# An attention and MLP kernel on one core: the first batch's attention in another order, the second batch's memory keys transposed early, one weight load cut in two

## The chip, the cores and the metric

The kernel runs on one core of a Trainium2 chip. The metric is device time in microseconds (us). Five engines work side by side, each through its own list of instructions in order, and they meet at semaphores only: TensorE (PE, with its weight loads shown as PEld), VectorE (DVE), ScalarE (ACT), GpSimd (POOL) and SyncE (SP). ACT, POOL and SP also issue DMAs, each on a queue of its own.

## The reference

Attention over chunks of 32 queries, each with 16 positions of left context, 8 of right context and 8 memory rows, for 4 batches, 8 heads, 768 positions, 64 values a head; then an MLP of 512 to 2048 to 512 with a "snake" function on the 3072 rows.

```python
for c in range(nc):                       # chunks of 32
    k_full = np.concatenate([mem_k, k_ctx], axis=2)
    v_full = np.concatenate([mem_v, v_ctx], axis=2)
    a = softmax(scale * q_c @ k_full.T)   # scale = 1/8
    out[:, :, c_start:c_end] = a @ v_full
x = out.transpose(0, 2, 1, 3).reshape(B * S, H * D)
h = x @ w_in
s = np.sin(alpha * h)
return (h + s * s / (alpha + 1e-09)) @ w_out
```

## The kernel before

All work is written out by hand in the tuple WORDS: five strings, one for the front and one for each of the four batches. A word is a letter and a number; method `do_<letter>` of the class Stage emits the instructions, and the order of the words is the order of the instructions on every engine. String 0 is the front: batch 0's attention alone. String i (from 1) is the MLP of batch i-1 with the attention of batch i woven in.

Words of the front that matter here, by head pair 0 to 3:

- `a` casts an f32 piece of q or k to bf16. Numbers 0 to 3 are k, 4 to 7 are q; the last letter is the engine, A for ACT (L700) and V for DVE (a tensor_tensor that takes the maximum of the piece with itself, L698). Pieces 0, 1, 2 of both come by ACT's and SP's queues (`load_f`, L762); piece 3 of both comes already cast by POOL's queue (`d`, L192).
- `l` and `k` transpose a q or k piece on PE into a bank of PSUM (12 instructions, L313); `L` and `K` copy it out on the named engine (L333, L324) and give the bank back.
- `s` is the scores of a head pair and half of the positions on PE (L351, L359), then their exponential on ACT (L366). `v` is the values (PE, L378), then the reciprocal of the sum and the product on DVE (L387, L388), which leave a tile x_blk.
- `T` and `t` transpose an x_blk on PE (L400) and copy it to xT, the MLP's input, on ACT (`T`) or DVE (`t`) (L403).
- `z` is one dummy matmul of 512 columns on PE (L733), `y` four of 128 columns (L739). `Ws` loads ACT's table for the sine (L752).
- `V`, `I`, `U`, `dq`, `dk`, `dm`, `dn` issue loads on POOL: values (L209, L216), w_in by tiles of 128 columns (L250), w_out (L256), the next batch's q and k (L192), memory values, and batch 1's memory keys (L713).
- `Ck` is const_k: 4 small PE transposes of the memory keys (L832), a copy to memkT (L836), and a copy into kT (L244). `n1` does the same for batch 1 later.

In the MLP strings `b` and `h` are the two halves of one of 16 tiles of the first layer (4 matmuls each, L462), `h` ends with the sine on ACT (L477), `q` squares it on the named engine (ACT L482, DVE and POOL L485), `g` finishes the tile on DVE (L489) and gives its two PSUM banks back, and `f` takes steps of the second layer (L500). `p0` and `P0` at the end of the front are the first three matmuls of the two halves of tile 0. PSUM has 8 banks of this kind, handed out in pairs or one by one by the class Banks as the words are run, so a PE instruction often waits for the engine that still reads its bank.

POOL's loads use eight semaphores in turn: each load waits until the one eight places ahead has landed.

Of the kernel before, what the change touches and what calls it, by code (L numbers as in the profile page):

```python
# [20 lines left out]

WORDS = (
    (
# [3 lines left out]
    ),  # L27
    (
# [93 lines left out]
def kernel(  # L122
# [12 lines left out]
    nc = tc.nc  # L135
# [5 lines left out]
    HP = H // 2  # L141
# [82 lines left out]
    def put_memv(b, eng=None):  # L224
        (eng or nc.vector.tensor_copy)(
            vws[b % 2][64:72, :, :, 0:D],
            memv_st[64:72, b, :, :].unsqueeze(2).to_broadcast([NM, H, NJ, D]),
        )
# [14 lines left out]
    def put_memk(b):  # L243
        nc.vector.tensor_copy(  # L244
            kTs[b % 2][:, :, 24:856].rearrange("p g (j c) -> p g j c", c=104)[:, :, :, 40:40 + NM],
            memkT[:, :, NM * b:NM * b + NM].unsqueeze(2).to_broadcast([P, HP, NJ, NM]),
        )
# [295 lines left out]
    class Stage:  # L543
# [137 lines left out]
        def do_m(self, a):  # L681
            put_memv(int(a))

        def do_n(self, a):
            const_k(int(a))

        def do_H(self, a):
            put_memv_heads(int(a))
# [67 lines left out]
    kq_f = [mlp.tile([P, 2, 6 * D], F32, name="kq_f", tag=t) for t in ("u", "s2") * 4]  # L756
# [4 lines left out]
    def load_f(ring, src, hp, t):  # L761
        ring.dma_start(  # L762
            t[:], src[0, 2 * hp:2 * hp + 2].rearrange("h (p r) d -> p h (r d)", p=P)
        )
# [3 lines left out]
    load_f(nc.sync, k, 0, kq_f[0])  # L768
    load_f(nc.scalar, q, 1, kq_f[HP + 1])
    nc.sync.dma_start(memk_f[0:NM], mem_k[0].rearrange("h n d -> n h d"))  # L770
    load_f(nc.scalar, q, 2, kq_f[HP + 2])
    load_f(nc.sync, k, 1, kq_f[1])
    load_f(nc.scalar, k, 2, kq_f[2])
    nc.sync.dma_start(alpha_rows[:], moe_alpha.rearrange("(ft p) -> ft p", p=P))
    nc.vector.memset(zeros[:], 0.0)
# [48 lines left out]
    def const_d():  # L824
        nc.vector.tensor_copy(memk_bf[0], memk_f[0:NM])

    def const_k(b=0):
        bank, bs = banks.single()
        a = memk_at[b]
        mt = bank[:, 0:2 * NM].bitcast(BF).rearrange("p (g c) -> p g c", g=HP)  # L830
        for g in range(HP):
            nc.tensor.transpose(  # L832
                mt[:, g, :], memk_bf[b][:, 2 * g:2 * g + 2, :].rearrange("p e d -> p (e d)"),
                ident[a:a + NM, a:a + NM]
            )
        nc.vector.tensor_copy(memkT[:, :, NM * b:NM * b + NM], mt)  # L836
        put_memk(b)
        banks.give(bs)

    def const_g():  # L840
        nc.vector.tensor_copy(memv_st[64:72, 0], memv_f[64:72])
# [22 lines left out]
    def const_s():  # L864
        nc.gpsimd.memset(kst[0:32, 0, :], 0.0)
        nc.gpsimd.memset(kst[96:128, NJ - 1, :], 0.0)

    consts_of = dict(b=const_b, d=const_d, g=const_g, c=const_c, m=const_m, i=const_i, k=const_k, l=const_l, p=const_p, v=const_v,
                     s=const_s, z=const_z)

# [36 lines left out]
```

## Time and profile before

| | |
|---|---|
| three runs | 213.85, 214.62, 214.97 us; median 214.62 |
| the profiled execution | 213.57 us, of which its span (first to last instruction) is 211.4 us |
| PE busy | 204.2 us (97%) |
| DVE, ACT, POOL busy | 139.6, 142.8, 100.7 us |
| POOL's queue of loads | 13.65 MB, 90.4% of the 16 DMA engines' time |
| first layer on PE (L462) | 512 matmuls, 326 ns each by the profile, one every 0.16 us |
| second layer on PE (L500) | 400 matmuls, 371 ns each by the profile |

A timeline row reads: start, length, engine, line, operation, output<-input, shapes, how many merged; in brackets the idle time of the engine ahead of it and what ended it. The times count from the span's start. A matmul's end is modelled: rows of matmuls overlap. In the rows of DMA issues the last number is the median time from issue to landing.

### The profile page before, as it was taken

Reading aid. Unit: us, or ns where it says so; the run is one execution under the profiler, and the core shown is the slowest. Engines: PE = TensorE matmul, PEld = TensorE weight load, DVE = VectorE, ACT = ScalarE, POOL = GpSimd, SP = SyncE. Lnnn points to the kernel's source line nnn. Section 1 sums busy time; section 2 is a strip of 40 time slices with the busy share of each in tenths; the row PEclk is TensorE's granted clock in tenths of the full one; section 3 lists DMA queues with packets and bytes.
Section 4 is the critical chain, followed back from the end, with each engine's and each line's share of the span. In section 5 each row is a group of like instructions: output and inputs, shape, how many; then the busy total and the mean of one; then the engine's idle time right before and its main releaser. Section 6 shows DMA issues by size and latency. Waiting matters only on the chain.

```text
span 211.4 us, 4539 instructions
## 1 busy us (share of the span) xinstructions
PE 204.2 (97%) x1754; PEld 116.8 (55%) x1754; DVE 139.6 (66%) x212; ACT 142.8 (68%) x228; POOL 100.7 (48%) x143
## 2 busy tenths in 40 slices
PE   7789999999999999999999999999999999999994
PEld 7467665656455555554456555554555555554443
DVE  7579698998363669957675569887347189964011
ACT  4499798959838579978827298968755198991110
POOL 8999518496696496029991058960000023300000
PEclk9999999999999999999999999999999999999999
DMA  6999999999999999999996569999246400000312
GB/s 212 308 138 137 211 207 203 205 163 178 167 162 131 165 142 150 99 142 157 159 201 120 82 175 133 131 137 88 102 105 109 136 0 0 5 0 0 149 53 99
DMA packets 95925, 27.81 MB, mean 132 GB/s; under 512 B 84880, under 2 KB 92448, under 8 KB 95904
## 3 DMA queue, kind: packets, MB, share of 16 engines
q0 software_dynamic: 69296, 13.65, 90.4%
q1 hardware_dynamic: 25520, 12.30, 29.7%
q10 hardware_dynamic: 1088, 1.57, 2.1%
q8 instruction: 14, 0.23, 0.5%
q14 instruction: 7, 0.06, 0.1%
HBM read 29.66 MB, written 6.29 MB: 170 GB/s over the span
## 4 chain that ended last, share of the span: by engine, by line
PE 83%; DVE 6%; ACT 4%; issue 2%; DMA 2%; POOL 1%; SPq 0%; DVEq 0%
PE ps L500 40%; PE ps L462 32%; PE ps L448 3%; PE ps L419 2%; PE ps L313 2%; DMA kq_f<-in_k_dram 2%; DVE gT L489 2%; DVE x_blk L388 2%; PE ps L400 1%; DVE s L485 1%; ACT u L477 1%; PE ps L733 1%; POOL s L485 1%; ACT s L482 1%; ACT pt L366 1%
## 5 line engine op out<-in xcount | busy, mean ns | idle before, releaser
L500 PE MATMUL ps<-w_out_sb,gT 128*128 128x512 bf16 (+2 forms) x400 | 89.0, 371 | 0.0
L462 PE MATMUL ps<-xT,w_in_sb 128*128 128x384 bf16 x512 | 86.4, 326 | 0.4 <-DVE gT L489 0.2
L489 DVE SCALAR_TENSOR_TENSOR gT<-s,inv_alpha,ps 128x768 bf16<-128x768 f32 x64 | 63.2, 1011 | 11.7 <-POOL s L485 5.3
L462 PEld LDWEIGHTS <-w_in_sb 128*128 128x128 bf16 x512 | 49.6, 98 | 35.4 <-issue 2.4
L477 ACT ACTIVATE u<-ps,alpha_sb 128x768 f32<-128x768 f32 x64 | 56.7, 896 | 18.1 <-PE ps L462 17.7
L500 PEld LDWEIGHTS <-gT 128*128 128x128 bf16 x400 | 36.6, 98 | 37.8 <-DVE gT L489 0.2
L485 POOL TENSOR_TENSOR s<-u 128x768 f32<-128x768 f32 x11 | 17.7, 1615 | 63.4 <-ACT u L477 50.8
L433 ACT ACTIVATE pt<-ps,biasm 128x256 bf16<-128x256 f32 x72 | 27.2, 490 | 10.5 <-PE ps L419 10.5
L507 DVE COPY o_sb<-ps 128x512 f32<-128x512 f32 (+1 forms) x15 | 10.1, 678 | 27.8 <-PE ps L500 25.9
L485 DVE TENSOR_TENSOR s<-u 128x768 f32<-128x768 f32 x24 | 22.8, 952 | 7.4 <-ACT u L477 7.4
L482 ACT ACTIVATE s<-u 128x768 f32<-128x768 f32 x29 | 24.2, 841 | 0.5
L388 DVE TENSOR_TENSOR x_blk<-ps,rinv 96x512 bf16<-96x512 f32 x32 | 22.0, 687 | 1.3 <-DVE rinv L387 0.2
L507 ACT COPY o_sb<-ps 128x512 f32<-128x512 f32 (+1 forms) x10 | 5.6, 562 | 22.2 <-PE ps L500 22.2
L387 DVE RECIPROCAL rinv<-ps 96x8 f32<-96x8 f32 x32 | 6.4, 199 | 13.3 <-PE ps L448 12.4
L209 POOL DMA_DIRECT2D vw<-in_v_dram x13 | 12.0, 923 | 5.1 <-PE ps L400 5.1
L216 POOL DMA_DIRECT2D vw<-in_v_dram x13 | 12.5, 958 | 1.1 <-issue 0.6
L275 POOL DMA_DIRECT2D kst<-in_k_dram x16 | 12.0, 748 | 1.6 <-DMA vw<-in_v_dram 0.7
L269 POOL DMA_DIRECT2D kst<-in_k_dram x16 | 11.1, 691 | 1.8 <-DMA vw<-in_v_dram 0.9
L403 ACT COPY xT<-ps 128x384 bf16<-128x384 bf16 x11 | 5.2, 497 | 8.0 <-PE ps L400 8.0
L282 POOL DMA_DIRECT2D q_bf<-in_q_dram x12 | 10.7, 905 | 0.0
L448 PEld LDWEIGHTS <-pt 128*128 128x128 bf16 x192 | 8.2, 97 | 4.2 <-ACT pt L433 0.3
L256 POOL DMA_DIRECT2D w_out_sb<-in_moe_w_out_dram x10 | 6.5, 649 | 6.9 <-DMA w_in_sb<-in_moe_w_in_dram 6.9
(82 smaller groups left out, 140.8 us busy)
## 6 DMA issues: line engine op xcount, KB each, us to landing
out_dram<-o_sb SPq DMA_DIRECT2D x23, 256.0 KB, 2.6
q_bf<-in_q_dram POOLq DMA_DIRECT2D x12, 128.0 KB, 5.1
kq_f<-in_q_dram ACTq DMA_DIRECT2D x3, 384.0 KB, 4.5
w_in_sb<-in_moe_w_in_dram POOLq DMA_DIRECT2D x1, 1152.0 KB, 12.9
vw<-in_v_dram POOLq DMA_DIRECT2D x8, 112.0 KB, 6.7
vw<-in_v_dram POOLq DMA_DIRECT2D x7, 128.0 KB, 6.5
kst<-in_k_dram POOLq DMA_DIRECT2D x14, 64.0 KB, 4.9
kst<-in_k_dram POOLq DMA_DIRECT2D x14, 56.0 KB, 5.0
```

The costliest lines, as they stand in the source:

```text
L209: nc.gpsimd.dma_start(vw[0:64, lo:c1, 0:D], win(vflat, a, n, 64))
L216: nc.gpsimd.dma_start(vw[72:128, c0:hi, 0:D], win(vflat, base + QW * c0 + 48, hi - c0, 56))
L388: nc.vector.tensor_tensor(out=x_blk[:].rearrange("p g e d -> p e g d"), in0=otv[0:QW, :, :, 0:D], in1=rinv[:].unsqueeze(3).to_broadcast([Q ...
L433: nc.scalar.activation(pt[:, 0:H * QW].rearrange("p (g e c) -> p g e c", g=2, e=4)[:, :, :, 32 * m:32 * m + 32], sc[:, :, 0:4 * QW].rearra ...
L448: nc.tensor.matmul(otv[:, e, hp, :], pt[:, QW * i:QW * i + P], vws[b % 2][:, 2 * hp + e, j, 0:D + 1],)
L462: nc.tensor.matmul(t["hT"][:, hf, 0:HALF], w_in_sb[:, kt, P * t["ft"]:P * t["ft"] + P], t["xT"][:, kt, HALF * hf:HALF * hf + HALF], start= ...
L477: nc.scalar.activation(t["u"][:], t["hT"][:, :, 0:HALF], ACTF.Sin, scale=alpha_sb[:, ft:ft + 1])
L482: nc.scalar.activation(s2[:], u[:], ACTF.Square)
L485: e.tensor_tensor(out=s2[:], in0=u[:], in1=u[:], op=ALU.mult)
L489: nc.vector.scalar_tensor_tensor(out=gT[:, ft, :].rearrange("p (e c) -> p e c", e=2), in0=t["s2"][:], scalar=inv_alpha[:, ft:ft + 1], in1= ...
L500: nc.tensor.matmul(o[:, c0:c1], gT[:, ft, P * s:P * s + P], w_out_sb[:, ft, c0:c1], start=(ft == 0), stop=(ft == FT - 1),)
L507: copier(state["engines"][state["o"] % len(state["engines"])])(o_sb[:, c0:c1], o[:, c0:c1])
```

## The change

Three things. In the front the words stand in another order: the casts of k1, k2 and q2 go from ACT to DVE; the copies L0, L1, L3 and K1 go from DVE to ACT, K2 from ACT to DVE; T00 goes from ACT to DVE as t00, t30 from DVE to ACT as T30, with the sine's table behind it; there are eight dummies `z` where there were four; k1's load goes to ACT's queue ahead of k2's, q2's to SP's. Batch 1's memory keys are loaded (`dn1`) and transposed (`j1`, new) in the front, so `n1` is only the copy into kT. The load of w_in's tiles 2 to 6 (`I27`) becomes `I24` and `I47`, with `dm` behind it, and the first tiles of the MLP of batch 0 run in the order 0 1 2 3 4 5 6 rather than 0 1 4 3 6 2 5.

```diff
 WORDS = (
     (
-        'y1 y1 y1 Ci y1 We y1 Cb y1 y2 y1 Cg m0 Cm dq068 a4A a0V a5A Cz dk068 l0 k0 z1 K0A V002 a1A Cd L0V l1 V024 a6A z1 '
-        'z1 Cp V046 Ck k1 Cv V068 a2A l2 s00 k2 L1V K2A l3 K1V s10 L2V s01 Cl s21 k3 L3V K3A v01 s11 dm v00 s31 I02 '
-        'v10 s30 Cs v11 s20 T10 v21 T01 I27 v20 z1 T00 T11 v30 T20 v31 p0 t21 t30 t31 P0 Ws '
+        'y1 y1 y1 Ci y1 We y1 Cb y1 y2 y1 Cg m0 Cm dq068 a4A a0V Cd a5A Cz dk068 dn1 l0 z2 k0 z1 l1 z1 V002 Ck a1V V024 K0A '
+        'L0A z2 s00 Cp a2V s01 V046 k1 Cv l3 k2 L1A V068 a6V K1A Cl k3 l2 K3A I02 s11 K2V L2V L3A I24 s10 j1 v00 s21 Cs '
+        'v01 z1 s20 I47 v11 t00 dm v10 s31 s30 v21 T11 v20 T10 T01 v30 z1 T20 v31 t21 T30 p0 t31 Ws P0 '
     ),
     (
-        'o8 b0 h0 I7g q0V U69 U12 b1 h1 dn1 dq108 q1A b4 h4 b3 g0 h3 b6 g1 dk108 q4V g4 q3A b2 h2 h6 b5 h5 Ufg g3 '
+        'o8 b0 h0 I7g q0V U69 U12 b1 h1 dq108 q1A b2 h2 b3 g0 h3 b4 g1 dk108 q2V g2 q3A b5 h5 h4 b6 h6 Ufg g3 '
...
         def do_n(self, a):
-            const_k(int(a))
+            put_memk(int(a))
+
+        def do_j(self, a):
+            turn_memk(int(a))
...
-    load_f(nc.scalar, q, 2, kq_f[HP + 2])
-    load_f(nc.sync, k, 1, kq_f[1])
+    load_f(nc.scalar, k, 1, kq_f[1])
+    load_f(nc.sync, q, 2, kq_f[HP + 2])
...
-    def const_k(b=0):
+    def turn_memk(b):
...
         nc.vector.tensor_copy(memkT[:, :, NM * b:NM * b + NM], mt)
-        put_memk(b)
         banks.give(bs)
+
+    def const_k():
+        turn_memk(0)
+        put_memk(0)
```

On ACT, in the front from the casts to the fourth exponential (the pt tiles), the rows before are these.

```order
L700 CAST q_bf<-kq_f 128x768 x2
L324 COPY kT_84<-ps 128x8x2x48
L700 CAST k_bf<-kq_f 128x768
L700 CAST q_bf<-kq_f 128x768
L700 CAST k_bf<-kq_f 128x768
L366 ACTIVATE pt_96<-ps 128x768
L324 COPY kT_84<-ps 128x8x2x48
L366 ACTIVATE pt_97<-ps 128x768
L366 ACTIVATE pt_98<-ps 128x768
L366 ACTIVATE pt_99<-ps 128x768
```

And after:

```order
L703 CAST q_bf<-kq_f 128x768 x2
L324 COPY kT_84<-ps 128x8x2x48
L333 COPY qT_86<-ps 128x768
L366 ACTIVATE pt_96<-ps 128x768
L366 ACTIVATE pt_97<-ps 128x768
L333 COPY qT_86<-ps 128x768
L324 COPY kT_84<-ps 128x8x2x48 x2
L366 ACTIVATE pt_98<-ps 128x768
L333 COPY qT_86<-ps 128x768
L366 ACTIVATE pt_99<-ps 128x768
```

Three casts have left ACT; behind the first exponential there stand four copies where there were two (one of before's two is further on).

On DVE the end of the front before, from the sixth x_blk to the first square of the MLP:

```order
L387 RECIPROCAL rinv<-ps 96x8
L388 TENSOR_TENSOR x_blk_95<-ps,rinv 96x2x4x64
L387 RECIPROCAL rinv<-ps 96x8
L388 TENSOR_TENSOR x_blk_92<-ps,rinv 96x2x4x64
L387 RECIPROCAL rinv<-ps 96x8
L388 TENSOR_TENSOR x_blk_90<-ps,rinv 96x2x4x64
L403 COPY xT<-ps 128x384 x3
L485 TENSOR_TENSOR s_587<-u 128x768
```

And after, from the third x_blk on:

```order
L388 TENSOR_TENSOR x_blk_92<-ps,rinv 96x2x4x64
L403 COPY xT<-ps 128x384
L387 RECIPROCAL rinv<-ps 96x8
L388 TENSOR_TENSOR x_blk_93<-ps,rinv 96x2x4x64
L387 RECIPROCAL rinv<-ps 96x8
L388 TENSOR_TENSOR x_blk_94<-ps,rinv 96x2x4x64
L387 RECIPROCAL rinv<-ps 96x8
L388 TENSOR_TENSOR x_blk_95<-ps,rinv 96x2x4x64
L387 RECIPROCAL rinv<-ps 96x8
L388 TENSOR_TENSOR x_blk_90<-ps,rinv 96x2x4x64
L387 RECIPROCAL rinv<-ps 96x8
L388 TENSOR_TENSOR x_blk_92<-ps,rinv 96x2x4x64
```

One copy to xT now stands inside the chain of the x_blk tiles, and behind the chain two are left rather than three; the third is on ACT, ahead of the sine's table.

On POOL, the loads between the values and w_in's last part:

```order
-L710 DMA memv_st<-in_mem_v_dram 8x24x64
-L250 DMA w_in_sb<-in_moe_w_in_dram 128x4x256
-L865 MEMSET kst 32x512
-L866 MEMSET kst 32x512
-L250 DMA w_in_sb<-in_moe_w_in_dram 128x4x640
+L250 DMA w_in_sb<-in_moe_w_in_dram 128x4x256 x2
+L871 MEMSET kst 32x512
+L872 MEMSET kst 32x512
+L250 DMA w_in_sb<-in_moe_w_in_dram 128x4x384
+L713 DMA memv_st<-in_mem_v_dram 8x24x64
 L250 DMA w_in_sb<-in_moe_w_in_dram 128x4x1152
```

The small load of the memory values has gone from ahead of w_in to behind its third part, and the middle part is two loads. (The number behind a tile's name is its buffer; after the change lines from 683 on stand 3 to 6 further down.)

2 rows, old and new, of the table WORDS are left out of this document.

## The prediction

> **What bounds the kernel now.** First the page: the span, PE's share, PE by slices, the chain.
>
> ```profile
> span 211.4 us, 4539 instructions
> PE   7789999999999999999999999999999999999994
> PEclk9999999999999999999999999999999999999999
> PE 83%; DVE 6%; ACT 4%; issue 2%; DMA 2%; POOL 1%; SPq 0%; DVEq 0%
> ```
>
> PE is nearly always busy, and the chain is PE for 83%. Busy time by stage tells where PE is not:
>
> ```profile
> 0.00:23.48 23.48, 19.57 (x322) 14.85 (x323) 17.77 (x49) 16.89 (x24) 21.80 (x52) 1.00 1.92 200
> 23.48:40.31 16.83, 16.82 (x105) 9.76 (x102) 14.19 (x18) 14.54 (x19) 7.60 (x9) 1.00 1.23 207
> 40.31:124.00 83.69, 83.56 (x766) 46.88 (x766) 56.65 (x84) 58.79 (x106) 50.34 (x66) 1.00 1.61 153
> 124.00:211.40 87.40, 84.21 (x569) 45.31 (x566) 50.99 (x65) 52.62 (x81) 20.92 (x17) 1.00 0.68 79
> ```
>
> (Stage, length, then busy PE, PEld, DVE, ACT, POOL.) From 23.48 to 124 PE idles 0.14 us. So the front is worth what it shifts the start of that unbroken run, less what the run can absorb. Then the timeline where the front ends and the MLP begins:
>
> ```profile
> 16.16 0.20 DVE L387 RECIPROCAL rinv<-ps 96x8 f32<-96x8 f32 x1 [0.71 <-ACT pt L366]
> 21.74 0.48 ACT L403 COPY xT<-ps 128x384 bf16<-128x384 bf16 x1 [0.22 <-PE ps L400]
> 22.24 1.28 ACT L752 ACT_TABLE_LOAD   x1
> 22.55 0.69 DVE L388 TENSOR_TENSOR x_blk<-ps,rinv 96x512 bf16<-96x512 f32 x1
> 23.16 0.88 DVE L403 COPY xT<-ps 128x384 bf16<-128x384 bf16 x3
> 23.48 16.91 PE L462 MATMUL ps<-xT,w_in_sb 128*128 128x384 bf16 x101
> 24.55 0.90 ACT L477 ACTIVATE u<-ps,alpha_sb 128x768 f32<-128x768 f32 x1 [0.81 <-PE ps L462]
> 25.48 0.96 DVE L485 TENSOR_TENSOR s<-u 128x768 f32<-128x768 f32 x1 [1.45 <-ACT u L477]
> 32.51 1.01 DVE L489 SCALAR_TENSOR_TENSOR gT<-s,inv_alpha,ps 128x768 bf16<-128x768 f32 x1
> 33.57 2.53 PEld L462 LDWEIGHTS <-w_in_sb 128*128 128x128 bf16 x16 [0.24 <-issue]
> 33.76 1.01 DVE L489 SCALAR_TENSOR_TENSOR gT<-s,inv_alpha,ps 128x768 bf16<-128x768 f32 x1 [0.24 <-POOL s L485]
> 35.26 2.86 DVE L489 SCALAR_TENSOR_TENSOR gT<-s,inv_alpha,ps 128x768 bf16<-128x768 f32 x3 [0.48 <-ACT s L482]
> ```
>
> DVE makes the eight x_blk from 16.16 to 23.24 (22.55 + 0.69), 0.88 a piece; PE starts 0.24 later. Then the first sine starts at 24.55, DVE squares from 25.48 and, with gaps of 0.1, is still at it at 33.52 (32.51 + 1.01): just then PE gets a pair of banks and goes on at 33.57. So to that point the first sine, through DVE, times PE.
>
> Last, the loads, from issue to landing:
>
> ```profile
> 13.89 0.89 POOL L216 DMA_DIRECT2D vw<-in_v_dram  x1
> vw<-in_v_dram POOLq DMA_DIRECT2D x1, 112.0 KB, 6.9
> 22.29 0.88 POOL L192 DMA_DIRECT2D k_bf<-in_k_dram  x1
> k_bf<-in_k_dram POOLq DMA_DIRECT2D x1, 768.0 KB, 18.9
> 20.96 0.41 PE L378 MATMUL ps<-vw,pt 128*128 128x65 bf16 x8
> 41.41 0.53 PE L313 MATMUL ps<-ident,k_bf 128*64 128x128 bf16 x12
> 42.06 3.46 PE L462 MATMUL ps<-xT,w_in_sb 128*128 128x384 bf16 x20
> ```
>
> The last values land at 20.8 and v30 starts at 20.96: that load held it. Batch 1's k lands at 41.2 and its transposes begin at 41.41. POOL's queue holds the same bytes ahead of both after the change (the memory keys of 8 KB come ahead of the values now), so I leave both landings where they are, 0.1 later for the first.
>
> **The change part by part.** The front's beginning and its unit prices:
>
> ```profile
> 8.30 0.85 PE L313 MATMUL ps<-ident,q_bf 128*64 128x128 bf16 x12
> 9.08 1.03 PE L733 MATMUL ps<-zeros 128*128 128x512 bf16 x2
> 10.04 0.18 PEld L832 LDWEIGHTS <-memv_st 8*128 8x128 bf16 x4 [0.84 <-issue]
> 10.56 0.23 DVE L244 COPY kT<-memkT 128x256 bf16<-128x256 bf16 x1
> 11.45 0.53 PE L313 MATMUL ps<-ident,q_bf 128*64 128x128 bf16 x12 [0.21 <-ACT q_bf L700]
> 11.91 0.34 PE L351 MATMUL ps<-mind,mrow 64*128 64x384 bf16 x2
> 12.46 0.81 ACT L366 ACTIVATE pt<-ps 128x768 bf16<-128x768 f32 x1 [0.33 <-PE ps L359]
> 15.97 0.79 ACT L324 COPY kT<-ps 128x768 bf16<-128x768 bf16 x1
> 19.66 0.86 ACT L403 COPY xT<-ps 128x384 bf16<-128x384 bf16 x2
> 5.96 0.96 DVE L698 TENSOR_TENSOR k_bf<-kq_f 128x768 bf16<-128x768 f32 x1 [0.37 <-DMA kq_f<-in_k_dram]
> ```
>
> *Scores start earlier: −1.4.* s00 starts at 11.91 because k1, l2 and their casts stand ahead. Now it needs the memory keys: their turn loses one of two dummies ahead (−0.45, half of what lies between 9.08 and 10.04) and comes at 9.6, its copy ends at 10.35 rather than 10.79, and behind the two new dummies s00 starts at about 10.5, its exponential at 11.05 rather than 12.46.
>
> *ACT behind it: +1.4 and two waits.* From 12.46 to its first xT copy at 19.66 ACT does ten operations, 0.72 each. Now twelve stand there (eight exponentials; L1, K1, K3, L3): 11.05 + 12 x 0.72 = 19.7, the old time. The banks add waits: v01 needs the bank of s10's exponential (end 16.8), and s20 stands behind v01 and a dummy on PE, so its exponential comes at 17.85 where ACT is free at 17.4 (0.48); s31 needs the bank of that one, and PE's turn and the way back leave ACT idle 0.6. The first xT copy (T11) comes at about 20.75, and v30 behind it on PE at 21.35, though its values landed at 20.9.
>
> *DVE: casts.* Three casts (0.96, of which 0.87 a step) start when the memory keys' copy ends, at 10.35, and with alpha, K2 and L2 fill DVE to 15.2. The copy of j1 waits for s11's exponential (15.4, the bank), so the first reciprocal comes at 16.1, no earlier than 16.16. The chain then holds the same eight at 0.85 (6.8), t00 (0.35) and the wait for v01 and v30 (0.4): last x_blk at 23.65, **+0.4**; the first layer starts 0.45 later.
>
> *T30 and the table on ACT.* Before, the table load followed T20 at 22.24. Now it stands behind T30, whose x_blk is v30's, ready at 22.8 (21.35, +0.55 for the matmuls and the way, +0.92 on DVE), 1.1 from there to the copy's end: 23.8. With 1.28 and a dummy activation (0.2) the first sine comes at 25.3, **+0.77**. Even if v30 waited for its load alone this would be +0.36 to +0.4.
>
> *DVE then carries it to PE.* The order of tiles does not alter DVE's list up to that point (square, two finishes, square, two, square, one), so PE's pair of banks comes at 34.3: **+0.76**.
>
> *The split load.* POOL's waits:
>
> ```profile
> POOL w_out_sb L256 <- DMA w_in_sb<-in_moe_w_in_dram: 6.9, 2, 5.4
> 32.18 1.55 POOL L485 TENSOR_TENSOR s<-u 128x768 f32<-128x768 f32 x1 [0.46 <-issue]
> ```
>
> POOL stood 5.4 us at a w_out load for w_in's last part, eight places ahead, so its square came at 32.18 and DVE idled 0.24 at 33.76. With one load more, what stands eight places ahead is the small one; the square is in time. DVE's next idle 0.48 waits for ACT, and stays. PE gets back what it stood after 33.57: 40.31 less 33.57 is 6.74 for 40 matmuls at 0.1625 = 6.5. I take 0.14 of the 0.24: **−0.14**. Splitting costs one issue on POOL (0.8), under a backlog of 6 us.
>
> *Batch 1's memory keys.*
>
> ```profile
> 48.48 0.18 PE ps L832 x4
> ```
>
> That is on the chain and goes: **−0.18**. In the front they cost PE 0.2 where it waits anyway.
>
> The sum: +0.76 −0.14 −0.18 = +0.44, on the profiled execution 213.57 to 214.0, on the median of 214.62 to 215.1. The profiled one is 1 us under the median, inside the runs' spread. About 0.5% (1.07 us) is what a measurement here can tell from nothing.
>
> [...]
>
> **The rivals.** (1) *The load alone holds the front.* If the waits I add on ACT and DVE do not show, v30 starts at 21.0, the first sine at 24.9 (+0.36): +0.36 −0.14 −0.18 = 0.0, 214.6. For it: 1.4 us of earlier scores; against: the banks. (2) *A faster front,* values landing a microsecond sooner or tile 0 in time. Then k's landing at 41.2 stops PE: its transposes can't begin before 41.22 (41.41 now), and tile 15 behind them starts at 41.55, not 42.06: −0.5 at most, with −0.18 it is 213.9. (3) *Slower for certain.* PE stays at its slow pace through the scores, since the front has fewer transposes early; it decides if 12 transposes still take 0.85 at 12.5. s00, s11, s20 and s31 then each add 0.2 to 0.3 on the way to ACT (0.53 against 0.85), 0.9 in all: +1.3, 215.9. Against it: four dummies more.
>
> **How the numbers follow.** Forecast (+0.2 to +0.8) 0.45; rival 1 0.27; rival 2 0.1; rival 3 or something like it 0.18. Beyond 1.07 us lie most of rival 3 and, with the runs' spread, parts of the forecast: slower 0.19. Rival 2 ends short of 1.07, so faster 0.1 is spread and what I overlook. The rest, 0.71, is the same. Range: from rival 2 (213.9) to rival 3 (215.9) and a little spread, 216.0.
>
> **What would show it.** Right: first exponential near 11; last x_blk 23.4 to 23.9; first sine 25.0 to 25.5; PE's stop for banks near 34.3; no 5 us wait of POOL at 31; no L832 near 48. Wrong: the sine before 24.6, or transposes of batch 1's k that wait for their landing at 41.2 (rival 2), or 12 transposes at 0.85 after 12 (rival 3).

## The result, and the profile after

The change is faster: 213.00 us (median of 11 runs) against 214.19 us (11 runs of the kernel before), ratio 0.9947 with a 95% interval of 0.9927 to 0.9967. I had forecast 0.44 us slower and a range that began at 213.9. The profiled execution took 212.98 us against 213.57. The comparisons further down leave out three slow executions, two of the kernel before (350 and 421 us) and, in the ratio, one of a_noz2 (216.68 us).

The page of the kernel after: span, PE and its granted clock by slices, the chain by engine.

```profile
span 210.9 us, 4551 instructions
PE   7989999999999999999999999999999999999994
PEclk9999999999999999999999999999999999999999
PE 73%; DVE 10%; ACT 6%; issue 4%; DMA 3%; SPq 1%; POOL 1%; DVEq 0%; ACTq 0%
```

Busy time by stage, with the stages of before (length, then PE, PEld, DVE, ACT, POOL):

```profile
0.00:23.48 23.48, 20.88 (x333) 15.39 (x334) 18.52 (x51) 16.27 (x24) 22.48 (x53) 1.00 1.72 206
23.48:40.31 16.83, 16.79 (x121) 10.00 (x120) 14.19 (x15) 15.46 (x20) 7.44 (x9) 1.00 1.23 206
40.31:124.00 83.69, 83.57 (x753) 46.59 (x748) 56.79 (x84) 58.83 (x107) 51.29 (x67) 1.00 1.65 152
```

PE was idle for 3.9 us of the first 23.48 us before and for 2.6 now. The timeline of the kernel after, at the places that the forecast named:

```profile
5.26 0.85 PE L313 MATMUL ps<-ident,q_bf 128*64 128x128 bf16 x12
6.04 0.91 PE L736 MATMUL ps<-zeros 128*128 128x512 bf16 x2
7.02 0.53 PE L313 MATMUL ps<-ident,k_bf 128*64 128x128 bf16 x12
9.97 1.51 ACT L366 ACTIVATE pt<-ps 128x768 bf16<-128x768 f32 x2 [0.89 <-PE ps L359]
14.98 0.20 DVE L387 RECIPROCAL rinv<-ps 96x8 f32<-96x8 f32 x1
16.87 0.81 ACT L366 ACTIVATE pt<-ps 128x768 bf16<-128x768 f32 x1 [0.46 <-PE ps L359]
18.27 1.51 ACT L366 ACTIVATE pt<-ps 128x768 bf16<-128x768 f32 x2 [0.60 <-PE ps L359]
21.92 0.69 DVE L388 TENSOR_TENSOR x_blk<-ps,rinv 96x512 bf16<-96x512 f32 x1
22.85 16.91 PE L462 MATMUL ps<-xT,w_in_sb 128*128 128x384 bf16 x101
24.09 0.88 ACT L477 ACTIVATE u<-ps,alpha_sb 128x768 f32<-128x768 f32 x1
31.54 1.58 POOL L485 TENSOR_TENSOR s<-u 128x768 f32<-128x768 f32 x1 [5.92 <-ACT u L477]
33.15 1.01 DVE L489 SCALAR_TENSOR_TENSOR gT<-s,inv_alpha,ps 128x768 bf16<-128x768 f32 x1 [0.24 <-POOL s L485]
40.79 0.53 PE L313 MATMUL ps<-ident,k_bf 128*64 128x128 bf16 x12
50.55 0.52 PE L419 MATMUL ps<-qT,kT 64*128 64x96 bf16 x16
166.39 3.90 PE L462 MATMUL ps<-xT,w_in_sb 128*128 128x384 bf16 x23 [0.31 <-DMA xT<-x_blk]
```

Twelve transposes take 0.53 us already at 7.02, where the kernel before took 0.85 until past 8.30. The first exponential starts at 9.97 (12.46 before), the first reciprocal, where DVE's chain of x_blk tiles begins, at 14.98 (16.16), the unbroken run of the first layer at 22.85 (23.48). So PE leads by 0.63 us; batch 1's first scores, at 50.55, lead by 0.88, the transposes of the memory keys having gone from in between:

```profile
48.41 0.25 PE L832 MATMUL ps<-ident,memv_st 8*128 8x8 bf16 x4
51.43 0.52 PE L419 MATMUL ps<-qT,kT 64*128 64x96 bf16 x16
```

(That is the timeline of before.) That quarter of a microsecond is no accident of this pair: from the run's start to those scores it is 27.95 or 27.96 us in all four traces with the keys transposed there, and 27.70 to 27.72 in all nine with them in the front. Near 166 us this execution loses 0.31 to a wait for batch 3's transposing DMA, which the profiled one of before did not have. −0.63 − 0.25 + 0.31 = −0.57, and the two executions differ by 0.59.

The medians differ by 1.19, twice as much. This pair does not show the other half; the next section does.

### The profile page after: what moved, and what is told of

Same layout as the page of the kernel before. It is cut to its first block, busy times and chain, and to the rows that moved or that the text cites. A ratio compares the mean times of both kernels' runs of the same rounds, so it can differ in the third digit from the quotient of the medians.

```text
span 210.9 us, 4551 instructions
## 1 busy us (share of the span) xinstructions
PE 204.6 (97%) x1758; PEld 116.8 (55%) x1758; DVE 139.7 (66%) x212; ACT 142.3 (67%) x228; POOL 101.2 (48%) x144
## 4 chain that ended last, share of the span: by engine, by line
PE 73%; DVE 10%; ACT 6%; issue 4%; DMA 3%; SPq 1%; POOL 1%; DVEq 0%; ACTq 0%
PE ps L500 37%; PE ps L462 27%; DVE gT L489 4%; DVE s L485 3%; PE ps L448 3%; PE ps L419 2%; DMA kq_f<-in_k_dram 2%; DVE x_blk L388 2%; ACT u L477 2%; PE ps L313 2%; DMA xT<-x_blk 1%; ACT qT L333 1%; PE ps L400 1%; POOL s L485 1%; DVE rinv L387 1%
## 5 line engine op out<-in xcount | busy, mean ns | idle before, releaser
L433 ACT ACTIVATE pt<-ps,biasm 128x256 bf16<-128x256 f32 x72 | 27.2, 489 | 10.5 <-PE ps L419 10.5
```

The source lines that it names most:

```text
L433: nc.scalar.activation(pt[:, 0:H * QW].rearrange("p (g e c) -> p g e c", g=2, e=4)[:, :, :, 32 * m:32 * m + 32], sc[:, :, 0:4 * QW].rearra ...
```

## The experiments

**What a second look at both kernels shows.** Each was run once more for a trace.

> The kernel before once more, for a second trace of it. If the earlier landings after the change (last values of batch 0 at 19.9 us after, at 20.8 before; batch 1's k at 40.4 and 41.2) are a matter of the execution and not of the change, this trace of before shows the first load of q landing at 3.9 rather than 4.36 us, or some other time up to 0.5 us off, and the values between 19.9 and 20.8. If they come from the change, the values land at 20.8 within 0.1 again. The slow pace of PE (12 transposes in 0.85 us) lasts to about 10.1 us again under either.

> The changed kernel once more, for a second trace of it. By the theory that the pace of PE made the front earlier, 12 transposes take 0.53 us from 7.0 us on again, the first exponential starts at 10.0 and the unbroken run of the first layer at 22.85, each within 0.1. If the loads decided, the landing of the last values (19.9) moves by up to 0.9 and the start of that run with it. The 0.31 us that PE waited near 166 us for a transposing DMA of batch 3 may be there or not.

The second trace of before took 215.36 us and shows a granted clock of 0.5 in the front. Here "half pace" is the state in which 12 transposes take 0.85 us, and "full pace" that in which they take 0.53. Windows of this trace, with borders where the granted clock changes and 3.41 us apart otherwise (length, then PE's busy time; the third number from the end is the granted clock):

```profile
0.65:4.06 3.41, 2.86 (x28) 2.86 (x29) 2.94 (x18) 1.22 (x1) 2.90 (x12) 1.00 0.59 184
4.06:7.47 3.41, 1.74 (x37) 1.31 (x35) 2.71 (x4) 1.91 (x4) 3.41 (x8) 1.00 1.04 364
7.47:10.89 3.42, 2.57 (x23) 1.05 (x23) 1.83 (x5) 1.76 (x4) 3.42 (x9) 0.50 1.23 268
10.89:14.30 3.41, 3.41 (x58) 2.81 (x58) 2.26 (x3) 2.44 (x4) 3.41 (x11) 0.50 2.78 150
```

The slow pace did not last to 10 us as I had expected under either theory: PE was at full pace from 4.06, lost it at 7.47 and had it again at 14.30. And the second trace of the changed kernel, 214.08 us:

```profile
5.35:15.59 10.24, 8.45 (x167) 5.64 (x169) 7.00 (x14) 8.06 (x11) 10.24 (x27) 1.00 1.83 227
15.59:19.00 3.41, 3.41 (x51) 2.41 (x47) 2.34 (x6) 1.62 (x2) 3.36 (x6) 0.50 2.88 147
```

Here too the trace did not repeat the first one within 0.1 us, as I had expected of the theory. At full pace from 5.35 the first exponential came at 9.52, not 10.0; then PE waited 0.83 us for a load of the values at 14.96, the window from 15.59 went at half pace, and the unbroken run started at 23.92, not 22.85:

```profile
9.52 1.51 ACT L366 ACTIVATE pt<-ps 128x768 bf16<-128x768 f32 x2 [0.81 <-PE ps L359]
23.92 0.33 PE L462 MATMUL ps<-xT,w_in_sb 128*128 128x384 bf16 x1
```

The stretches between two recorded changes last 3.41 and 6.83 us in c_before (4.06 to 7.47 to 14.30) and 10.24 and 3.41 in c_after (5.35 to 15.59 to 19.00): 3.41, or two or three times as much. So I cut the traces into windows of 3.41 us and set PE's busy share in each against its pace in the next. The first profiled pair, in the same cut:

```profile
3.39:6.81 3.42, 2.73 (x31) 2.28 (x28) 2.95 (x7) 1.92 (x4) 3.42 (x9) 1.00 1.06 370
6.81:10.22 3.41, 3.24 (x31) 1.63 (x31) 1.39 (x3) 1.90 (x3) 3.41 (x5) 1.00 1.16 300
```

is before, where PE came to full pace at 10.22, after 3.24 busy of 3.41 but not after 2.73; and

```profile
3.29:6.70 3.41, 3.41 (x34) 2.51 (x31) 2.89 (x8) 2.18 (x4) 3.35 (x10) 1.00 1.06 368
6.70:10.11 3.41, 3.35 (x53) 1.79 (x52) 1.85 (x6) 1.98 (x4) 3.41 (x5) 1.00 1.17 300
```

is after, where it came at 6.70. The column reads 1.00 in both kernels from the start, while the first recorded change stands at 10.22 and at 6.70 and 12 transposes ahead of it took 0.85 us: I had taken that 1.00 for full pace. In the fronts of the thirteen traces of this case the lowest busy share of a half-pace window that full pace followed was 84% (c_before, 2.86 us of the 3.41 from 0.65), and the highest that it did not follow 80% (before, 2.73 of 3.42 from 3.39). Of the windows at full pace the highest share that half pace followed was 60% (a_castsA, 2.03 of 3.41 from 7.79), the lowest that it did not follow 63% (a_fill, 2.14 of 3.41 from 4.72). At the end of the kernel, where PE has only the second layer's matmuls, it was otherwise: windows of 49 to 58% in five traces were still followed by full pace (in a_again 1.69 us of the 3.41 from 206.85). So the busy share does not tell all, and what else counts stays open. The borders lie at another time in each execution (first recorded change at 10.22 in before, 6.70 in after, 4.06 in c_before, 5.35 in c_after).

The landings moved too, within one kernel: k of batch 1 at 41.17 and 40.83 us in the two of before, 40.45 and 41.06 in the two of after; the last values at 20.82 and 20.47, 19.90 and 20.22. Differences as in the first pair occur without the change.

What a half-pace window costs is read from the runs, whose mean granted clock is listed: one recorded window is 0.5 of 3.41 in 211 us, 0.008. Half pace ahead of the first record does not show in that figure (a_mlp0: half pace until 7.24, clock 1.000), so even the first column can hold slow starts. The three comparisons below, each on another chip, have 64 executions of the kernel before:

| kernel | clock 0.998 to 1.000 | 0.991 or 0.992 | 0.982 to 0.984 |
|---|---|---|---|
| before | 27 runs, mean 213.86 us | 28 runs, 214.69 | 9 runs, 215.04 |
| changed, first comparison and a_again | 23 runs, 213.22 | none | none |

So over half of the executions of before show one or two slow windows and are 0.8 or 1.2 us longer, the mean of all being 214.39: 0.53 above those without. The changed kernel had one such execution in 24, c_after. At equal clock it gains 0.64. 0.53 and 0.64 add up to the difference of these means, 1.17; the first comparison, with other executions of before, measured 1.19. Whether the windows cost the time, or only come with late loads that do, the table can't tell; b_fill below tests it.

**The dummies between l0 and k0.** In the changed order they were taken out, in the old one put in. (These are passages of WORDS, here and below; ... stands for words left out.)

```diff
-dk068 dn1 l0 z2 k0 z1 l1 z1        (a_noz2, from the changed kernel)
+dk068 dn1 l0 k0 z1 l1 z1
-dk068 l0 k0 z1 K0A                 (b_z2, from the kernel before)
+dk068 l0 z2 k0 z1 K0A
```

> The changed kernel without the two dummy matmuls between l0 and k0. Theory A (they close PE's idle 0.9 to 1.2 us at 6 us, so that PE takes its fast pace at 6.8 and not at 10.1, and all of the front hangs on that): 12 transposes take 0.85 us until about 10, the scores of s00 start at 10.2 to 10.5 rather than 9.3, the last x_blk ends 0.7 to 1.1 later than 22.6, PE's unbroken run starts at 23.5 to 23.9; the time is 0.7 to 1.0 us over the changed kernel's, 0.997 to 1.001 of before. Theory B (the new order of casts and copies, or loads that landed sooner, gave it whatever PE's pace): s00 within 0.4 of 9.3, since the memory keys still turn behind the same loads, the run starts by 23.1, and the time stays at 0.994 to 0.996 of before.

> The kernel before with two dummy matmuls put between l0 and k0, nothing else. Theory A: PE is fast (12 transposes in 0.53) from about 7 us. But here s00 waits for ACT's cast of q2 at 11.4 us, which waits for loads and two casts ahead and not for PE, so s00 starts at 11.8 to 11.95, the front ends where it did, and the time is 0.999 to 1.001 of before. Rival (the fast pace is worth its 0.6 us in any order): the front ends 0.4 to 0.7 sooner, 0.997 of before.

a_noz2: 0.9998 (0.9961 to 1.0035); 6 of 12 executions had a slow window or two. Its trace:

```profile
5.70:9.11 3.41, 1.13 (x24) 0.65 (x21) 1.55 (x2) 1.12 (x2) 3.41 (x8) 1.00 1.09 343
9.11:12.52 3.41, 3.41 (x35) 1.62 (x37) 1.87 (x4) 1.39 (x3) 3.35 (x12) 0.50 1.81 175
```

PE was busy for a third of one window and at half pace in the next; the first exponential came at 12.34, the first layer's run at 25.21. k0's load landed at 7.21 here, 1.2 later than in the first trace of the changed kernel, so this trace alone does not tell what the dummies did; the twelve executions do. Without the two dummies no gain over the kernel before can be measured. Theory A had the time right, but "slow until about 10" was too simple: in this execution PE had been at full pace from 5.70 and lost it. One thing stays open: of the six executions without a recorded slow window four took 212.90 to 213.61, as the changed kernel does, and two took 214.63 and 215.55, and none of the two was traced.

b_z2: 1.0006 (0.9976 to 1.0037), 8 of 12 with a slow window, so the same two dummies bring nothing measurable in the old order, as theory A had it. Its timeline tells why:

```profile
10.46 0.53 PE L313 MATMUL ps<-ident,k_bf 128*64 128x128 bf16 x12 [1.52 <-ACT k_bf L700]
11.19 0.53 PE L313 MATMUL ps<-ident,q_bf 128*64 128x128 bf16 x12 [0.21 <-ACT q_bf L700]
12.40 0.85 PE L313 MATMUL ps<-ident,k_bf 128*64 128x128 bf16 x12
```

PE is at full pace early, runs out of work sooner, waits 1.52 us for a cast (1.68 busy of the 3.41 from 8.23), and has lost its pace at 12.40.

**All the idle of the front filled.** Nine dummies more in the old order (b_fill), four more in the new one (a_fill, run again as a_fill2), and b_fill with batch 1's memory keys moved (b_fill_j1).

```diff
-dk068 l0 k0 z1 ... V046 Ck k1 Cv ... s01 Cl s21        (b_fill)
+dk068 l0 z2 k0 z1 ... V046 Ck z5 k1 Cv ... s01 Cl z2 s21
-dk068 l0 z2 k0 z1 ... s01 Cl z2 s21 ... b1 h1 dn1      (b_fill_j1, from b_fill)
+dk068 dn1 l0 z2 k0 z1 ... s01 Cl z1 j1 z1 s21 ... b1 h1
-I24 s10 j1 v00 s21 Cs v01 z1                           (a_fill, a_fill2)
+I24 s10 z2 j1 z1 v00 s21 Cs z1 v01 z1
```

> The kernel before with nine more dummy matmuls where PE waits in the front: two between l0 and k0, five ahead of k1, two ahead of s21; nothing else. If the pace of PE is the gain, wherever it comes from (windows kept above 0.8), this reaches 0.996 to 0.998 of before, with 0 to 2 executions of 12 at 0.992. If pace is worth something only in the new order (before, s00 waits for casts behind loads until 11.4 us), the slow windows become fewer but the median stays at 0.998 to 1.002, and a trace with no slow window after 7 us has its unbroken run start at 23.2 to 23.5, no sooner than before.

> The kernel before with nine more dummies as in b_fill (one of the two ahead of s21 stands behind j1), and batch 1's memory keys loaded and transposed in the front; the old order of casts and copies, the old w_in loads and tiles. If windows at half pace and the memory keys are all that the change gave: 0.992 to 0.9965 of before, within 0.3 us of the changed kernel, and PE's lead grows by 0.25 us between 45 and 51 us against before. Rival (the new order of casts and copies gives the rest): 0.3 to 0.6 us over the changed kernel, 0.9965 to 0.998.

> The changed kernel with four more dummy matmuls where PE waits: two ahead of j1, one behind it, one ahead of v01. By theory A no window after the first full one falls under 0.76, so all 12 executions show a mean clock of 0.999 or more, and the median is that of the changed kernel less 0.1 to 0.5 us, 0.991 to 0.996 of before. If dummies delay v00 and v01 (0.2 us each) more than they save: up to 0.2 us slower than the changed kernel.

> The changed kernel with four more dummies where PE waits, as a_fill. If its 212.74 us of six runs hold: 0.991 to 0.9945 of before, all executions with a mean clock of 0.998 or more. If they were chance: as the changed kernel, 0.9945, with the clock at 1.0 too, since the changed kernel shows hardly a slow window as it is.

> The changed kernel once more, in rounds. The traces so far show PE's pace decided anew every 3.41 us, at a phase that differs from execution to execution: half pace for the next 3.41 us when PE had been busy for 33 to 58% of the last (in full pace) or for no more than 80% (in half pace). Theory A (windows): the front's time depends on that phase, and each window at half pace costs 0.6 to 1.1 us; after the change fewer executions have one than before, where 10 of 22 had a mean clock of 0.992 or less. So 0 to 4 of these 12 have one, and the median is 0.993 to 0.997 of before. Rival (the change is faster by its order and by batch 1's memory keys alone, 0.5 to 0.9 us, whatever the pace): as many executions at 0.992 as before, and the same ratio between executions of equal clock.

| | ratio to before | 95% interval | median, us | executions with a slow window |
|---|---|---|---|---|
| changed kernel again (a_again) | 0.9945 | 0.9925 to 0.9966 | 213.21 | 0 of 12 |
| b_fill | 0.9957 | 0.9935 to 0.9978 | 213.58 | 0 of 12 |
| b_fill_j1 | 0.9971 | 0.9953 to 0.9989 | 213.61 | 0 of 12 |
| a_fill | 0.9927 | 0.9901 to 0.9953 | 212.74 | 0 of 6 |
| a_fill2 | 0.9941 | 0.9921 to 0.9961 | 212.93 | 0 of 9 |

Dummies alone, in the old order, take all recorded slow windows away and make before 0.92 us faster by the ratio (0.0043 of 214.5), a little more than I had expected. Its loads and their order are those of before, so it is the filled waits that do it. Most of the change's gain is thus reached without the new order. b_fill's profiled execution is not faster than that of before, whose run started at 23.48; it is the others that gain:

```profile
10.34 0.83 ACT L700 CAST k_bf<-kq_f 128x768 bf16<-128x768 f32 x1 [1.68 <-DMA kq_f<-in_k_dram]
12.97 0.81 ACT L366 ACTIVATE pt<-ps 128x768 bf16<-128x768 f32 x1 [0.33 <-PE ps L359]
23.75 6.50 PE L462 MATMUL ps<-xT,w_in_sb 128*128 128x384 bf16 x39
```

At full pace from 5.53 us on, the old order still starts the first exponential 2.6 us after the start of k1's cast, and that cast waits for its load. b_fill_j1 starts its run at 23.26, its load having come 0.66 sooner, and its lead over b_fill grows from 0.48 at 44 us to 0.73 at 74: the 0.25 of the memory keys is there in the trace. In the medians it is not (213.61 and 213.58), and I can't say whether it is lost behind 74 us or in the spread; two sets of 12 runs that spread over a microsecond, on two chips, don't tell a quarter of one apart. So the rest of the change, the new order of casts and copies above all, is worth about 0.4 us over the old order with dummies: 213.63 to 213.22 in the means of 24 and 23 runs, the uncertainty of either mean being some 0.1. The 0.64 at equal clock are then 0.23 that the old order with dummies gives as well, and 0.41 of that rest. For b_fill_j1 the rival won: 0.9971 lies in its range and outside mine, by which windows and keys were all; only PE's growing lead was as I had said.

Four more dummies in the new order: 0.9927 and 0.9941, against 0.9947 and 0.9945. It is the fastest version measured, but its lead over the changed kernel, 0.1 to 0.5 us, is inside the intervals.

**The engine of the casts.**

```diff
-Ck a1V V024 K0A L0A z2 s00 Cp a2V s01 ... V068 a6V K1A
+Ck a1A V024 K0A L0A z2 s00 Cp a2A s01 ... V068 a6A K1A
```

> The changed kernel with the casts of k1, k2 and q2 on ACT again, at the same places of the order. My forecast had them on DVE as a cost that ends at 15.2 us and fills DVE. If instead they are what frees ACT for the first scores: ACT's copies of k0 and q0 stand behind a cast whose load lands at 9.3 to 10.2, so s00 starts at 11.3 to 12.2 rather than 9.6, PE has an idle of 1.5 us or more ahead of it, half of the executions show a mean clock of 0.992, and the time is 1.0 to 2.5 us over the changed kernel's (0.999 to 1.006 of before). Rival (the engine of the casts does not matter once PE keeps its pace): within 0.4 us of the changed kernel, 0.993 to 0.997.

1.0082 (1.0056 to 1.0108), 216.09 us: 2.9 us over the changed kernel, the largest effect of all and more than the 1.0 to 2.5 that I had expected. From its timeline:

```profile
8.87 0.83 ACT L703 CAST k_bf<-kq_f 128x768 bf16<-128x768 f32 x1 [1.39 <-DMA kq_f<-in_k_dram]
9.60 0.79 ACT L324 COPY kT<-ps 128x768 bf16<-128x768 bf16 x1
11.68 0.81 ACT L366 ACTIVATE pt<-ps 128x768 bf16<-128x768 f32 x1 [0.58 <-PE ps L359]
26.01 4.23 PE L462 MATMUL ps<-xT,w_in_sb 128*128 128x384 bf16 x25
```

The copy of k0, whose transposes on PE ended before 8, stands behind a cast that waits for its load, the first exponential comes 1.7 us later than in the changed kernel, and the two casts behind it delay ACT's next exponentials and copies. The run starts 3.2 us later; a window at half pace, from 11.20 to 14.61, is in that. It is not what makes the time long, as far as four executions tell: of them two have no slow window and took 215.84 and 216.24 us, the two others 215.94 and 216.28. Moving the casts to DVE is what makes room for the early scores; I had counted it as a cost of DVE only.

**The split load and the tiles.** w_in's middle part as one load again, the memory values ahead of it, the old order of tiles.

```diff
-L3A I24 s10 ... s20 I47 v11 t00 dm v10 ... b2 h2 b3 g0 h3 b4
+L3A dm s10 ... s20 I27 v11 t00 v10 ... b4 h4 b3 g0 h3 b6
```

> The changed kernel with w_in's middle part as one load again, the memory values ahead of it, and the first MLP's tiles in the order of before. My term of -0.14 for the split: POOL stands 5 us at the w_out load and its square comes late, DVE idles 0.24, PE's run from the first sine to batch 1's transposes is 0.1 to 0.24 longer. What the traces of both kernels now say (POOL's square comes 8.0 us after the unbroken run's start in both, 31.54 less 22.85 and 32.18 less 23.48 being 8.69 and 8.70, since it waits for its sine either way): POOL stands at that load again, but the run from its start to the first of batch 1's q transposes stays at 16.83 us, and the split and the order of tiles are worth nothing.

One execution, 214.03 us, no recorded slow window, though the pace was half until 7.24. From the run's start to batch 1's transposes it is 23.52 to 40.36: 16.84, against 16.83 in both kernels, and 16.83 to 16.85 in every other trace, with the split or without it. The split is worth nothing there. (The long wait did not come back: POOL stood 1.6 us at the load, not 5, as the loads eight places apart were others.) Its front was 0.67 later than the changed kernel's for another reason, and one that I had in the forecast:

```profile
21.00 0.41 PE L378 MATMUL ps<-vw,pt 128*128 128x65 bf16 x8 [0.48 <-DMA vw<-in_v_dram]
```

Here the last values, landed at 20.87, did hold v30. In one execution that is no proof that the load order does it.

## Why the prediction was wrong

By its own steps:

- *Scores start earlier, −1.4.* The step that failed. I had the slow pace last until 10 as before, by the rows of one execution (12 transposes in 0.85 us at 8.30, in 0.53 at 11.45), and put the first exponential at 11.05; it came at 9.97. The two dummies between l0 and k0, which I counted among the eight without asking what idle they fill, keep the window from 3.29 to 6.70 full (before, the one from 3.39 was busy for 2.73 of 3.41), and PE takes its full pace 3.5 us sooner. The memory keys turn at 8.58, where I had 9.6, and s00 starts at 9.30, where I had 10.5.
- *ACT behind it, and DVE.* The walk from there was right but for that 1.1: waits of 0.48 and 0.6 on ACT forecast, 0.46 and 0.60 measured; first xT copy at 20.75, it came at 19.67; last x_blk at 23.65, it ended at 22.61; first sine at 25.3, it started at 24.09. "No earlier than 16.16" for the first reciprocal fell with it: 14.98.
- *T30 and the table, +0.77 at the first sine, and +0.76 at PE.* The steps were right, their start was not. The sine came 0.46 earlier than before, not 0.77 later: the same walk 1.1 us sooner, and 1.48 rather than 1.65 from the last x_blk to the sine. PE's run came 0.63 earlier, and its pair of banks at 32.97 rather than 34.3 (33.57 before).
- *The split load, −0.14.* Wrong by itself: POOL's square starts 8.69 us after the run in the changed kernel and 8.70 before (31.54 less 22.85, 32.18 less 23.48). It waits for its sine; the 5.4 us at the load ended just ahead of that, and DVE's 0.24 is still there at 33.15.
- *Batch 1's memory keys, −0.18.* Right in kind; −0.25 in the traces, the matmuls around it included.
- *Landings left where they are.* They differ between executions: the last values landed at 19.90 to 20.87 in the thirteen traces, at 19.90, 20.22 and 20.27 in the three of the changed kernel. So neither 20.8 nor 41.2 was a bound. The cap of the second rival, 213.9, rested on them. Its sign, a sine before 24.6, did come, but by PE's pace.
- *The base.* I set the sum against one profiled execution, 213.57, and called the median's 1 us above it spread. It was of the kind without a recorded slow window, 27 of 64 executions in the later comparisons; the 0.53 us by which the mean lies above that kind can't be seen in that trace at all. This half of the gain was in no term of the sum.

## What to carry to other kernels

Where the first microseconds of a kernel are full of short waits, look at PE's busy share between the recorded changes of the granted clock (here in stretches of 3.41 us), in several traces: dummy matmuls in the waits can be worth more than a better order (here 0.9 us against some 0.4), and the four placed where PE waited anyway showed no cost in a_fill and a_fill2 (0.9927 and 0.9941 of before, the changed kernel 0.9947 and 0.9945). Compare runs of equal mean granted clock, and say which class the profiled execution belongs to before a sum is set against it. In a_castsA a cast that waited 1.39 us for its load held up ACT's copies behind it, and the first exponential came at 11.68 rather than 9.97: put such a cast on an engine whose next work is not needed sooner.

## What was not expected of the hardware

A granted clock of 1.00 at the start went with half pace in both profiled executions: 12 transposes took 0.85 us at 8.30 in before and at 5.26 in after, ahead of the first recorded change (10.22 and 6.70), and 0.53 behind it, at 11.45 and 7.02. The first load of q, issued at 0.75 us in all thirteen traces, landed between 3.90 and 4.54. PE's wait for the transposing DMA of batch 3 near 166 us was nothing and 0.7 us in two traces of before, 0.2, 0.3 and 0.6 in three of the changed kernel, and is part of the runs' spread.
